# Three staging buffers moved and a new hand-made order in a fused attention, expert and channel-mix chain

## The chip, the cores and the metric

The kernel runs on one core of one Trainium2 chip. The metric is device time in microseconds of one execution; lower is better. Three executions of the kernel before took 497.76, 499.23 and 499.36 us, so the median is 499.23 us. One more execution was recorded by the hardware profiler, and all rows below are from that one.

## What is computed

Three blocks run one after the other on four sequences. The first is attention with 8 heads: 512 local tokens that see a window of 32 on each side and 32 global tokens, and 32 global tokens that see everything. Its output (576 tokens of 512 features) feeds four causal attention experts with a top-2 gate. Their sum feeds a channel mix with a sigmoid gate:

```python
x = concat(out_g, out_l)                       # block 1
logits = x @ w_gate                            # block 2: top-2 of 4 experts
q, k, v = x @ wq[e], x @ wk[e], x @ wv[e]
ye = softmax(causal(scale * q @ k.T)) @ v @ wo[e]
out += mask[..., None] * w[:, :, kk:kk+1] * ye
xk = mu_k * x + (1 - mu_k) * x_prev            # block 3
xr = mu_r * x + (1 - mu_r) * x_prev
k = maximum(xk @ w_k, 0)
result = sigmoid(xr @ w_r) * (k * k @ w_v)
```

## The kernel before

Products that need more than one pass of TensorE's rounded float are done with operands split into a high and a low half (H and L), three matmuls for one (`mm3`, line 161 and after). The halves are made by a copy on ScalarE or VectorE (the high half) and a subtraction on GpSimd or VectorE (the low half).

Block 1 has 32 units `n`, two for each of 16 pairs of heads. A unit is: `a_qk` (line 289) with sixteen matmuls `S`, four reductions on VectorE and four exponentials on ScalarE; `a_norm` (line 319) with a reciprocal `rc` on VectorE and three multiplications on GpSimd that make `pn` and `glob`; `a_tp` (line 338) with four transposes `pT` and a copy of them. Four units make a group `u`; `a_pv` (line 423) forms the group's output `x{u}0` and `x{u}1` with the values `vw`, and two groups are one sequence, held in `xT[b]`. The global queries are in `g_qk` and its followers (`Sga`, `Sgb`, `pTG`, `pTh`, `xg`, `pTx`). Inputs of a pair come as one `kq` tile, four of which fit.

Block 2 starts with projections. `load_wb` (line 239) fetches raw wq, wk and wv into a staging tile, and `split_wb` (line 250) makes their halves. `b_split` (line 448) makes the halves of `xT[b]` in a tile with the tag `x`; `b_qk` and `b_v` (lines 464 and 493) then do the projections, `pb{b}{ep}{q or k}{half}` and `pv{b}{i}`. All three raw tiles and the halves of `xT[b]` have the tag `x`, which has one buffer, so each of them has to be used up before the next can be fetched or written. After that come score tiles `C`, transposes `cT` and outputs `y`.

Block 3 folds the output weights into w_k and w_r (`g_make`, line 755: `Gr` and `Gk`), where the raw w_k and w_v arrive in quarter tiles through three staging tags in turn (`load_half`, line 221: tags `ql`, `mask`, `csm1`) and are split by `narrow_block` (line 188). The gate's sigmoids are computed early (`r`, `rl`) and parked in DRAM as `rd0` to `rd16`. Then four passes of `d_k` (tiles `k`, halves `kk`) and `d_v` (tiles `v`) run, and `d_out` (line 851) fetches a parked sigmoid into a tile `ro{n}{i}`, multiplies it with `v{n}{i}` and writes the product out. The last pass has five such tiles; they use the tags `wy` and `wg` by turns, with two buffers each, so three of the five share the two buffers of `wy`.

Nothing is scheduled by a library. Every call is recorded, and `Log.emit` (line 99) replays the record in the sequence of the table `ORDER`; the table `SLOTS` says which buffer of its tag, and which of the eight PSUM banks, each tile gets. So each engine executes its instructions in the sequence of that table, and a tile waits for the readers of the tile that had its buffer before. Every instruction has line 105, that of the replay.

Of the kernel before, what the change touches and what calls it, by code (L numbers as in the profile page):

```python
# [19 lines left out]
DM = H * HD  # L20
# [5 lines left out]
NC = DM // 128  # L26
# [91 lines left out]
def chain_kernel(ctx: ExitStack, tc: tile.TileContext, kq, vw, vgd, wqkv, wo, pack, w_k, w_v, w_r, c_causal, out):  # L118
# [82 lines left out]
    wy = {"n": 0}  # L201
# [649 lines left out]
    def d_out(n, i, pv):  # L851
        r = T(("wy", "wg")[i % 2], [DM], f"ro{n}{i}")
# [151 lines left out]
def sequence(text):  # L1004
    n = 0
    for word in text.split():
# [8 lines left out]
15 -7 12 -11x2 -14 10 2 -13 -2 26x6 -15 -10 7 -15 22 -22 10 3 -19 16 -5 -10x2 -4 19 576 -577 90 -29x8 1703 -1733x8 120  # L1015
-163x9 1 -2 -21 22 189x8 -196 -4 20 -20 2x8 -34 24 10 1 -2 2 11 -14 14 65 -80 14 37x8 -44 -6 19 1 -21 21 -35 101x8 -96
21 -20 -27 24 117x8 -124 92 3 -85 -13 39 68 -64 99 -103 -44 12 27 32x8 -35 -33 131 -100 -32 72 -63 20 -8 55 -59 53
-37x8 -16 -5 171 -168 47 -8 -121 123 3 -33 41 -41 -2 2 28 115 -152 -44x4 44 -54 83 -84 53 -73 124 -83 79 -105 8 92
-20x4 20 33 -141 103 31 -23x5 22 -141 29x4 -29 84 17 -3 11x4 -13 -25 -52 75 25 -15 -78 65 47x32 -50 -18 -13 30 -43 35
-12 -56 72x2 -71 115x2 -47 -40 43 -5x2 5x4 35 -42 61 -66 48x8 -53 61 -58 72x8 -97 63 1 -71 77 -7 8x4 -134 149 256x8  # L1020
-310 22 5 16 -23 28 -41 4 44x4 -111 97 -4 15x3 -12x4 -13 195x8 -234 27 7 -41 36 3 196 1 -206 23x8 -25 201 -212 208
-361 211x8 -100 107 -64 156x8 -224 122 -37 28 7 -40 31x2 6 -38 -3 -6 1 -2 43 -48 34 -31 4 30 -24x4 -21 20 -10x4 -6 28
-24 161x8 -151 -25 136 -126 128 -166 156 -120 127 -166 157 -125 127 -204x4 38 -39x3 300x8 -68 -50 9 42 -111x40 -87 -52
156 114 -90 28 -47 111 -66 -27 86 -79x8 -40 -24 -4 46 19 -39x4 -28 65 -153x4 155 -46 9 151 -195 74 -154 155x4 -77 -5
114x4 -16 -29 -55 170 -53 -60 -160x32 48 67 -177 246 -43 -29 -6 34 40 -138 113 -20 42 4 -10 -30x4 22 7 273 -352 81 -53
117x4 200 -270 -37 -161x2 146 116 -201 115 58x8 -57 -41 40 -41 -150 189 79x8 -279 301 -122 101 -133 151 -7x4 -153 136
# [36 lines left out]
122 60 -61x2 2 -3 2 -3 2x2 -48 84x2 10 -96 11 73x2 539 -629 47x12 -13 38 13 532 -537 140 -9 -209 -21 236 -90x3 -64 -66
129x3 -56 -42 208 -249 -2 132 4x4 108 -375 -2 127 605 -762x12 391 359 -2 -359 -375 733 -471 110 -258 -101x12 133 -182
144 608 -617 617 -464 -72 -173x12 232 -275 202 -176 -48 275 -229 41x12 652 -694 232 -233 233 459 -653x12 -14 192 -193
322x2 -243 185x4 53 -246 194x6 -198 188 -195 5 235x2 -241 199 -42x4 -231 308 -78 -232 248x4 15 -204 167 -69x6 59 -160
219x6 -44 -83 1 85 -88 96 -164x12 142 -87 122 -281 252 -27 54 -2 -227x12 161 55 -286 229 -129 183 -3 -54 -129 128
# [43 lines left out]

SLOTS = {
    "vC": "010100101",
    "kp": "10320321023120130123",
    "blk": "120102120120120",
    "bank": (
        "050534124535534141120326706341754527434545237344417313235256072171150256716757622557117214376540"
# [101 lines left out]
```

## Time and profile before

| | us |
|---|---|
| median of 3 executions | 499.23 |
| the profiled execution | 496.65 |
| its span, first to last instruction | 494.8 |
| TensorE busy in it | 470.3 (95%) |
| VectorE, ScalarE, GpSimd busy | 311.8, 284.1, 265.8 |
| bytes moved by DMA | 48.4 MB |

TensorE is busy for 95% of the span at a mean granted clock of 0.998 of full speed. The busy time counts modelled ends of matmuls, so short waits can hide in it. The other engines are busy for 54% to 63% of the span, but not evenly: for the first third they are close to full, and for the last quarter nearly empty.

### The profile page before, as it was taken

The page shows a single profiled execution, that of the slowest core. Times are in us where ns is not written, and L with a number is a line of the kernel's source. Part 1 is how long each engine was busy: PE and PEld are TensorE (multiplying, and loading weights), DVE is VectorE, ACT ScalarE, POOL GpSimd, SP SyncE. Part 2 cuts the span into 40 slices and gives each one's busy share as a digit, 9 for nine tenths or more (in the row PEclk, how much of TensorE's full clock was granted, in tenths as well). Part 3 has the DMA queues.
Part 4 walks back from the last instruction along what each step waited for, and adds up shares of the span by engine and source line. Part 5 has one row for each costly group of instructions (what it writes and reads, how often), then busy time and mean ns, then how long its engine had stood idle before and what let it go on. Part 6 is the DMA issues. An engine that isn't in the chain of part 4 may idle for free.

```text
span 494.8 us, 11667 instructions
## 1 busy us (share of the span) xinstructions
PE 470.3 (95%) x4238; PEld 399.3 (81%) x4238; DVE 311.8 (63%) x1126; ACT 284.1 (57%) x863; POOL 265.8 (54%) x389
## 2 busy tenths in 40 slices
PE   6798989999999999999999998998999999999994
PEld 5466778887988897997777786987989889989883
DVE  3887857997597667788767659987735125314222
ACT  4988986786567567668755756565422213214210
POOL 2978767476738756875856125686451332223240
PEclk9999999999999999999999999999999999999999
DMA  8947770040200000101022574412215013004003
GB/s 328 411 154 259 273 290 31 2 143 12 86 1 2 1 2 3 44 2 42 23 66 83 194 253 150 144 51 86 84 46 167 1 56 116 0 1 149 23 0 127
DMA packets 19369, 48.36 MB, mean 98 GB/s; under 512 B 2160, under 2 KB 2800, under 8 KB 19312
## 3 DMA queue, kind: packets, MB, share of 16 engines
q1 hardware_dynamic: 19024, 47.36, 27.5%
q8 instruction: 33, 0.54, 0.5%
q10 hardware_dynamic: 288, 0.26, 0.2%
q14 instruction: 24, 0.20, 0.1%
HBM read 38.70 MB, written 8.91 MB: 96 GB/s over the span
## 4 chain that ended last, share of the span: by engine, by line
PE 68%; DMA 11%; DVE 9%; ACT 4%; POOL 3%; issue 2%; SPq 0%; DVEq 0%; POOLq 0%; ACTq 0%
PE v L105 17%; DMA kq<-in_kq_dram 5%; PE pv L105 5%; PE cT L105 4%; PE y L105 4%; PE C L105 4%; PE x L105 3%; DMA rawk<-in_moe_w_k_dram 2%; PE S L105 2%; DMA vw<-in_vw_dram 2%; DVE rawv L105 2%; POOL wv L105 1%; PE pT L105 1%; DMA rawv<-in_moe_w_v_dram 1%; DVE rawk L105 1%
## 5 line engine op out<-in xcount | busy, mean ns | idle before, releaser
L105 PE MATMUL v<-wv,kk 128*128 128x512 f32 x408 | 98.0, 391 | 1.5 <-POOL wv L105 1.5
L105 POOL TENSOR_TENSOR kk<-k,kk 128x512 fp32r<-128x512 f32 (+1 forms) x32 | 44.9, 1410 | 87.2 <-ACT kk L105 82.6
L105 PEld LDWEIGHTS v<-wv,kk 128*128 128x128 f32 x408 | 74.9, 188 | 16.0 <-POOL wv L105 1.8
L105 ACT ACTIVATE sm<-sm,mn 128x160 f32<-128x160 f32 x128 | 53.6, 423 | 10.2 <-DVE mn L105 9.9
L105 POOL TENSOR_TENSOR pn<-sm,rc 128x256 f32<-128x256 f32 x64 | 38.6, 626 | 22.1 <-DVE mng L105 8.4
L105 ACT CAST kk<-k 128x512 fp32r<-128x512 f32 (+1 forms) x32 | 20.6, 649 | 50.7 <-PE v L105 37.1
L105 POOL TENSOR_TENSOR csm<-csm,crc 128x128 f32<-128x128 f32 (+3 forms) x64 | 46.9, 754 | 1.3
L105 DVE CUSTOM_DVE_ANT_0 sm<-S,band 128x160 f32<-128x160 f32 x128 | 35.6, 317 | 19.1 <-PE S L105 16.7
L105 ACT ACTIVATE csm<-csm,cmn 128x256 f32<-128x256 f32 (+3 forms) x64 | 35.9, 562 | 9.8 <-DVE cmn L105 5.9
L105 DVE TENSOR_TENSOR ro<-v,ro 128x512 f32<-128x512 f32 x17 | 11.6, 690 | 42.3 <-PE v L105 39.6
L105 DVE SCALAR_TENSOR_TENSOR k<-k 128x512 f32<-128x512 f32 (+1 forms) x32 | 28.7, 911 | 14.1 <-ACT k L105 13.5
L105 DVE CUSTOM_DVE_ANT_0 csm<-C,causal 128x128 f32<-128x128 f32 (+3 forms) x64 | 29.6, 486 | 6.4 <-PE C L105 2.5
L105 PE MATMUL S<-kq 64*64 64x160 f32 x512 | 25.2, 306 | 5.5 <-DMA kq<-in_kq_dram 3.8
L105 PEld LDWEIGHTS S<-kq 64*64 64x64 f32 x512 | 17.4, 132 | 14.0 <-DVE rc L105 3.9
L105 POOL TENSOR_TENSOR wk<-yk,wk 128x256 fp32r<-128x256 f32 x16 | 12.7, 797 | 29.3 <-ACT wk L105 29.3
L105 POOL TENSOR_TENSOR x<-xT,x 128x256 fp32r<-128x256 f32 (+1 forms) x32 | 22.4, 726 | 10.6 <-ACT x L105 10.6
L105 PE MATMUL pv<-wv,x 128*128 128x260 f32 x192 | 25.2, 286 | 0.0
L105 ACT ACTIVATION_READ_ACCUMULATOR sm<-sm,mn 128x1 f32 x128 | 24.6, 192 | 0.0
L105 PEld LDWEIGHTS pv<-wv,x 128*128 128x128 f32 x192 | 23.7, 188 | 0.7 <-DVE cmn L105 0.4
L105 PE MATMUL cT<-ident,csm 128*128 128x128 f32 x160 | 23.7, 279 | 0.0
L105 POOL TENSOR_TENSOR wv<-yv,wv 128x256 fp32r<-128x256 f32 x16 | 16.8, 1066 | 12.4 <-ACT wv L105 9.1
L105 PE MATMUL C<-qk 64*128 64x384 f32 (+3 forms) x192 | 22.4, 349 | 0.0
(901 smaller groups left out, 1270.8 us busy)
## 6 DMA issues: line engine op xcount, KB each, us to landing
kq<-in_kq_dram SPq DMA_DIRECT2D x15, 688.0 KB, 7.6
vw<-in_vw_dram SPq DMA_DIRECT2D x16, 512.0 KB, 10.5
ro<-rd SPq DMA_DIRECT2D x17, 256.0 KB, 2.9
rawk<-in_moe_w_k_dram SPq DMA_DIRECT2D x16, 256.0 KB, 3.5
rd<-rt SPq DMA_DIRECT2D x16, 256.0 KB, 3.5
rawv<-in_moe_w_v_dram SPq DMA_DIRECT2D x16, 256.0 KB, 2.7
out_dram<-ro SPq DMA_DIRECT2D x16, 256.0 KB, 2.1
rawr<-in_moe_w_r_dram SPq DMA_DIRECT2D x4, 512.0 KB, 3.8
```

Of the source, the lines that this page charges most:

```text
L105: getattr(getattr(self.nc, engine), name)(*[now(x) for x in args], **{k: now(x) for k, x in kwargs.items()})
```

## The change

Two tiles change their tag, and the two tables are replaced as a whole. The matmuls, the operations of the other engines and the DMAs are the same in number and kind.

```diff
-        raw = T("x", [NC, w], f"raww{kind}")
+        raw = T(("x", "d3", "qk")[step], [NC, w], f"raww{kind}")
...
-        r = T(("wy", "wg")[i % 2], [DM], f"ro{n}{i}")
+        r = T(("wy", "wg", "wy", "wg", "ql")[i], [DM], f"ro{n}{i}")
...
 ORDER = """
-15 -7 12 -11x2 -14 10 2 -13 -2 26x6 -15 -10 7 -15 22 -22 10 3 -19 16 -5 -10x2 -4 19 576 -577 90 -29x8 1703 -1733x8 120
+0 14 -14 19 -10 -13 26x6 -7 -14 -3 -2 4 -14 16 -15 11 -14 15 -18 2 17 -18 8 -9 9 582 -580 -14 106 -29x8 -29x8 21 1 -2
...
 SLOTS = {
-    "kp": "10320321023120130123",
+    "kp": "20310123132032101320",
```

The tag `d3` is otherwise used by the raw w_r and by a tile of block 3, `qk` (three buffers) by a transposed tile of block 1 and by the projections, `ql` by a small tile of block 2 and by the raw w_k and w_v. On the DMA queue of SyncE, raw wv is now the twelfth transfer instead of the 27th, ahead of the second round of `kq` tiles, and raw wk the 29th instead of the 20th.

The first place is TensorE's queue between the transposes of the global weights `pTg2` and the unit `S16`, the first that reads a tile of the third round of `kq`. Before (`pT` and `pTg` are transposes, `x1` the output of group 1):

```order
L105 MATMUL pT10_842<-ident_90,pn10_741 128x128 x4
L105 MATMUL pTg2_850<-ident_90,glob2_666 128x128 x4
L105 MATMUL x10_866<-pt1_513,vw2_203 64x64 x16
L105 MATMUL x11_883<-pt1_513,vw2_203 64x64 x16
L105 MATMUL pT11_922<-ident_90,pn11_839 128x128 x4
L105 MATMUL pT13_936<-ident_90,pn13_909 128x128 x4
L105 MATMUL x10_866<-tg1_680,vgb_145 128x512
L105 MATMUL x11_883<-tg1_680,vgb_145 128x512
L105 MATMUL S16_0_951<-kq8_823 64x160
```

And now, where `pb` and `pv` are projections of the first half of sequence 0:

```order
L105 MATMUL pTg2_898<-ident_137,glob2_719 128x128 x4
L105 MATMUL pb00q0_909<-x00_744,wq_304 128x256 x12
L105 MATMUL pT10_929<-ident_137,pn10_865 128x128 x4
L105 MATMUL pb01q0_942<-x00_744,wq_304 128x256 x12
L105 MATMUL pT11_968<-ident_137,pn11_894 128x128 x4
L105 MATMUL pv01_976<-wv_490,x00_744 128x260 x12
L105 MATMUL pT13_998<-ident_137,pn13_966 128x128 x4
L105 MATMUL pv00_1004<-wv_490,x00_744 128x260 x12
L105 MATMUL pTG11_1036<-ident_137,gl_114 128x128 x4
L105 MATMUL pTG10_1048<-ident_137,gl_114 128x128 x4
L105 MATMUL pTh10_1056<-ident_137,gl_114 128x128
L105 MATMUL pTh11_1059<-ident_137,gl_114 128x128
```

The next row there is `S16`. Four projections, 48 matmuls, have come in between units of block 1; they stood after `S24` and later. The outputs `x10` and `x11` stand ahead of this piece now.

The second place is TensorE's queue where the folded weights `Gk` end and the first `k` tiles begin, in block 3. `Gk01` is read by the `c` matmuls, `Gk0s` by the `a` matmuls. Before:

```order
L105 MATMUL Gk011_5075<-wk00_4711,wok_4600 128x512 x6
L105 MATMUL Gk011_5075<-wk02_4705,wok_4600 128x512 x3
L105 MATMUL Gk011_5075<-wk03_4593,wok_4600 128x512 x3
L105 MATMUL Gk01s_5105<-wk00_4711,wos_3783 128x512 x6
L105 MATMUL Gk01s_5105<-wk02_4705,wos_3783 128x512 x3
L105 MATMUL Gk01s_5105<-wk03_4593,wos_3783 128x512 x3
L105 MATMUL k00c_5137<-dH0_3063,Gk01_5089 128x256
```

Now, on the same engine (of `r31c`, `r30a` and `r31a` the second halves, which read alike, are left out, and of `Gk01s` the last two rows):

```order
L105 MATMUL Gk011_5014<-wk03_4552,wok_4720 128x512 x3
L105 MATMUL r31c_5044<-Gr01_4324,dH3_4354 128x512 x2
L105 MATMUL r31c_5044<-Gr01_4324,dL3_4439 128x512
L105 MATMUL r30a_4834<-Gr00_4560,dH3_4354 128x512 x2
L105 MATMUL r30a_4834<-Gr00_4560,dL3_4439 128x512
L105 MATMUL Gk00s_5069<-wk00_4694,wos_4314 128x512 x6
L105 MATMUL Gk00s_5069<-wk02_4766,wos_4314 128x512 x3
L105 MATMUL Gk00s_5069<-wk03_4552,wos_4314 128x512 x3
L105 MATMUL r31a_4976<-Gr00_4560,dH3_4354 128x512 x2
L105 MATMUL r31a_4976<-Gr00_4560,dL3_4439 128x512
L105 MATMUL Gk01s_5106<-wk00_4694,wos_4314 128x512 x6
L105 MATMUL k01c_5140<-dH0_3151,Gk01_5031 128x256
```

Between the last matmul of `Gk011` and the first `c` matmul stood one group of twelve 128x512 matmuls; now there are two such groups (`Gk00s`, `Gk01s`) and three groups of six (`r31c`, `r30a`, `r31a`).

The third place is the end of SyncE's DMA queue. Before:

```order
L105 DMA ro30_6530<-rd12_81 128x512
L105 DMA ro33_6540<-rd15_84 128x512
L105 DMA ro34_6550<-rd16_85 128x512
L105 DMA out_0_dram<-ro23_6194 128x512
L105 DMA ro31_6614<-rd13_82 128x512
L105 DMA out_0_dram<-ro30_6530 128x512
L105 DMA out_0_dram<-ro31_6614 128x512
L105 DMA out_0_dram<-ro33_6540 128x512
L105 DMA ro32_6800<-rd14_83 128x512
L105 DMA out_0_dram<-ro34_6550 64x512 x2
L105 DMA out_0_dram<-ro32_6800 128x512
```

Now:

```order
L105 DMA ro33_6499<-rd15_84 128x512
L105 DMA out_0_dram<-ro23_6254 128x512
L105 DMA ro31_6645<-rd13_82 128x512
L105 DMA out_0_dram<-ro30_6470 128x512
L105 DMA out_0_dram<-ro31_6645 128x512
L105 DMA out_0_dram<-ro32_6488 128x512
L105 DMA out_0_dram<-ro33_6499 128x512
L105 DMA out_0_dram<-ro34_5660 64x512 x2
```

The fetch of `ro32` from among the last writes is gone: it now stands with those of `ro30` and `ro33`, while `ro34` is fetched into the tag `ql` as the 97th of the 133 transfers, between raw quarter tiles of w_v.

## Rows read from the trace of the kernel before

**Rows 1.** Stretches: us; PE, PEld, DVE, ACT, POOL busy; clock; DMA share; GB/s

```profile
0.00:47.00 47.00, 36.89 (x635) 26.61 (x639) 33.28 (x204) 38.45 (x151) 33.13 (x68) 1.00 0.75 282
47.00:120.00 73.00, 69.68 (x1203) 58.37 (x1196) 56.68 (x284) 57.12 (x211) 48.24 (x84) 1.00 0.38 141
120.00:300.00 180.00, 179.81 (x1352) 151.22 (x1351) 131.06 (x466) 122.25 (x350) 108.08 (x178) 1.00 0.18 57
300.00:360.00 60.00, 56.18 (x339) 49.66 (x338) 48.62 (x103) 34.44 (x86) 38.56 (x34) 1.00 0.31 101
...
487.80:494.80 7.00, 0.00 (x0) 0.00 (x0) 1.41 (x3) 0.00 (x0) 0.00 (x0) 0.86 0.48 163
```

**Rows 2.** Waits of PE: what waited for what, us in total, times, longest

```profile
PE S L105 <- DMA kq<-in_kq_dram: 3.8, 5, 1.1
PE k00c L105 <- POOL Gk L105: 1.6, 1, 1.6
...
PE v L105 <- POOL wv L105: 1.5, 1, 1.5
PE x L105 <- issue: 1.5, 1, 1.5
...
PE xg L105 <- ACT gl L105: 0.7, 1, 0.7
PE pTg L105 <- POOL glob L105: 0.6, 1, 0.6
```

**Rows 3.** Timeline of the end: start, us, engine, operation, tiles, count [idle before]

```profile
479.69 8.10 PE L105 MATMUL v<-wv,kk 128*128 128x512 f32 x35
...
487.14 1.37 DVE L105 TENSOR_TENSOR ro<-v,ro 128x512 f32<-128x512 f32 x2 [0.67 <-PE v L105]
488.29 0.38 SPq L105 DMA_DIRECT2D ro<-rd  x1
...
491.21 0.69 DVE L105 TENSOR_TENSOR ro<-v,ro 128x512 f32<-128x512 f32 x1 [2.69 <-DMA ro<-rd]
...
491.93 0.34 SPq L105 DMA_DIRECT2D out_dram<-ro  x1
```

**Rows 4.** DMA issues from 488.6 us: count, KB each, median us to landing

```profile
out_dram<-ro SPq DMA_DIRECT2D x2, 128.0 KB, 2.7
out_dram<-ro SPq DMA_DIRECT2D x1, 256.0 KB, 2.0
```

**Rows 5.** Timeline of PE from 43 to 47 us

```profile
43.35 1.09 PE L105 MATMUL pT<-ident,pn 128*128 128x128 f32 x8
44.37 1.13 PE L105 MATMUL x<-tg,vgb 64*128 64x512 f32 x4
46.63 0.64 PE L105 MATMUL S<-kq 64*64 64x160 f32 x12 [1.13 <-DMA kq<-in_kq_dram]
```

**Rows 6.** Timeline of PE from 60 to 70 us: the first projection

```profile
68.06 1.68 PE L105 MATMUL pb00k<-x,wk 128*128 128x256 f32 x12
```

**Rows 7.** POOL by shape, 0 to 47 us: busy, mean ns, idle before

```profile
L105 POOL TENSOR_TENSOR pn<-sm,rc 128x256 f32<-128x256 f32 x27 | 16.1, 616 | 10.3 <-DVE mng L105 8.4 <-DVE rc L105 1.4 <-ACT pt L105 0.5
L105 POOL TENSOR_TENSOR glob<-sm,rc 128x128 f32<-128x128 f32 x13 | 5.2, 403 | 0.0
L105 POOL TENSOR_TENSOR gl<-gl,rcg 128x544 f32<-128x544 f32 x4 | 4.4, 1097 | 0.8 <-DVE rc L105 0.8
L105 POOL TENSOR_TENSOR wq<-rawwq,wq 128x256 fp32r<-128x256 f32 x4 | 2.9, 734 | 0.0
```

**Rows 8.** Timeline of POOL: its first and last operations of that stretch

```profile
12.83 1.19 POOL L105 TENSOR_TENSOR pn<-sm,rc 128x256 f32<-128x256 f32 x2 [8.38 <-DVE mng L105]
...
43.61 0.40 POOL L105 TENSOR_TENSOR glob<-sm,rc 128x128 f32<-128x128 f32 x1
```

**Rows 9.** Timeline: PE's last Gk group, and POOL's low halves of w_v

```profile
303.42 2.88 PE L105 MATMUL Gk01s<-wk,wos 128*128 128x512 f32 x12
...
342.37 4.60 POOL L105 TENSOR_TENSOR wv<-yv,wv 128x256 fp32r<-128x256 f32 x3 [3.04 <-ACT wv L105]
```

More of the change, by code (lines that the diff above doesn't have):

```diff
@@ new lines @@
+2 -78 211x8 -141 -4 94 -94 -77 77 139 1555 -1555 -197x8 18 1 -2 170 -64 -107 2 103 -129 24 103 -126 138x8 312 -463 4
+-31x8 18 6 120 -124 14 169 -133x8 -65 127 -127 97x8 -25 -64 -34 196 -141 105 -163 163 -108 -41 148 16 -126 -64 153
+-30x8 -135 208 -206 61 72 -137 99x8 -38 -7 -67 138 -5 55 -58 -131 201 -50 -73 118 -69 -96 98 -4 -96 48 221 -241 -31 48
+221 -228 78 12x4 -42 -98 138 -88x4 54 -110 215 -162 -34x4 15 8 18 56 -79 22 -46 112x4 26 2 -124 15 151 -48 -128 129
+-31 27 -106 35x4 -62 77 -85 28 40 -3 67 70x4 -104 104 -206 134x32 39 -3 20 241 -242 241 -475 232 275 -438 17 148x4
@@ new lines @@
+-154 18 135 265 -420 179x4 -30 -3 -152 80x2 100 -243 -5 63 119x8 -190 62 81 -52 54x8 288 -351 48 49 -5 -95 157x8 -208
+137 -32 29 -94 66 -61x4 54 -67 97 -30 97 -101 4 96 -74 2 -30 100 47x40 -194 -4 230x8 -230 187 83 -332 152 178 -285
+206x8 74 -250 67 4 -52x8 253 -210 -5 106 -3 -104 2 105 -134x4 -89 215 -104 -25 -80x4 89 -106 115 -101 28x4 274 -275
+149x2 55x8 -187 382 1 -2 -193 -192 -4 196 -197 -8 9 193 -32 -173 173 -164 161 -173 50x32 -74 165 -93x2 -84 128 -129
+166 222 -219 -44 62 -192 214x8 -21 -120 64 101x8 -109 -68 69 239 -164 -56x8 -15 225 -4 -218 -24 74 4 35 52 -94 -33
@@ new lines @@
+-42x4 234 -263 17 42 -148x4 271 -119 -154 193x4 -115 10 54 -46 5 430x12 -403 3 60 -5 -56x4 56 10 -83 82 -31 453x12
+-518 82 -17 -54 59 3 -45 -85 124 -33x4 32 -50 4 319x12 -296 4 -30 -17 48 -15 76 -192 195x4 -84 163x12 -206 38 66 1200
+-1194 -8 -74 -34 1307 -1201 219 -192 9x4 217 940 -1309 203 -55 -38x4 20 67 -88 209 -178 216 -252 -31x8 -94 117 358
+-327 1153 -978x8 -335 476 -274x8 -115 38 -44 4x2 18x8 11 -43 -2 1212 -1261x32 17 7 -5 25 -446 448 -4x2 9 -7 -2 205
+-205 84 -140x2 135 -88 82 125 2 -122 -46 207x8 -49 -122 -46 158 -112 -143 256 -126 -36 211x8 -63 -295x4 353 -319 464
@@ new lines @@
+-137 100 96 34 -35 34 -32x12 -78 -100 161 -34 -258 90 233 -98 63 -292 256 -141 -117 103x3 150 66 -66 43 -158x12 100 1
+-75 -80 196 -118 137 -88 -44x12 -49 130 -51 -81 80 -14 -66 -3 2 -3 -93 282x3 -148 -138 19x12 -31 136 32 -119 -50 167
+112 -232 367x12 -314 -116 250 -136 138 -3 3 -2 -230 61x4 161 -227 65 44x4 286 -337 164 -26x2 -139 133x2 -89 196x4
+-200x2 285 -159x3 -219 287 84 -96x4 7 -71 67 -228 134 39x6 41 92 -375 177x6 -124 314 -371 -5 287x6 -234 124 55 -56
+404x6 -414 58 -4 192 -432 182 248 -432 618x6 -193 -195 358 -165 -142 -168 115 51 -165x10 -138 240 -240 292 298 -592
@@ new lines @@
+593 -594 291 -292 589 -590x3 619 -387 -70 -49 293x6 -255 126 -160 104 385 -386 53 -173 426x4 -430 171 -7 34 228
+-226x10 284 3x2 -338 337 -261 -154x4 119 216 -187 212 -242 241 -258 -17x12 48 -24 -21 44 -154 203 -99 -104 120 80
+-16x2 -115x12 -84 -5 101 88 -63 273 -301 47 40x2 -159x12 41 105 -194 87 111 -199 330 -182x12 37 133 -332 41 230 -231
+206x3 -93 113 -307x12 415 -121 -23 -139 -2 281 -120 -117 92x3 -140 302 -405x12 -48 138 156 144 -441 275 94x4 66 -261
+260 23x3 -284 189 94x3 -290 182x4 -183 -2 -140 480x4 -162 -323 133 94x4 -93 208x10 66 58 -64 -189 -98 258 -93x6 50 130
@@ new lines @@
+134x6 -140 -49 211x13 -36 -2 251x6 -139 -83 -36 89 33x7 -95 -87x6 175 -24 23 -274x12 24x3 31 -32x3 29 -30x6 55x2 243x6
+-249 86x6 -92 -35x3 123 -92 174 -208x9 24x3 31 -32x3 29 -30x6 85x6 -33 -35x3 65 -34 -33x3 342x6 -348x3 345 -346x3
+133x6 210x6 -215 -117x3 329 -314x6 251x6 -251 1 -31x3 276 36x6 -291 -29x3 26 295 -323x3 321 -160x7 -27 -119x15 104
+-102x3 -5 41 -35x3 -5 36 -43 49x6 -45 -6 144x6 -95 -51 51 122x6 37x6 -43 104 -286x3 226 -109 101x6 -85 -93 -49 298
+-123x6 43 -226 47 177 99x6 -40 8x6 -119 -79x6 36 -104x3 65x2 -67x3 231 -232x6 121x6 -69 26x6 37 -70 69 255x6 -299
@@ L1109 @@
+33 -34x9 25x18 3x3 -5 7x3 -5 -6 12x3 -5 -6 12x3 -5 -6 10 -6 5x2
 """
@@ L1140 @@
-    "qk": "012011120102120",
+        "210020110212201002021010121200200121012120210002212200011002210102002012001011021222201010210100"
+        "12101201002112"
+    ),
+    "cpt": "10010101011010011010011010",
+    "mng": "10011001",
+    "sug": "01101001",
+    "wg": "01000000110001011011011001101011001",
+    "rcg": "01101001",
+    "qk": "1020122020120102",
     "lg": "0000",
     "gate2": "0101",
-    "cmn": "01202100120121102202210102100122",
-    "csu": "01202100210212022112001210200211",
@@ L1145 @@
-    "crc": "02101202101201202102011210200211",
+    "cmn": "00121020202101100212002112012201",
+    "csu": "02101012201001222201001221202120",
+    "crc": "01202012101010222210220110210102",
 }
```

189 lines of the change are left out of this document (77 added, 112 removed).

## The prediction

> **What bounds the kernel now.** I read the table of stretches first. It says that TensorE sets the time nearly everywhere: between 120 and 300 us it idles for 0.2 of 180 us, and between 360 and 487.8 us not at all, at a granted clock of 1.00 [rows 1]. The idle time stands in four places: 47.00 − 36.89 = 10.1 us in the first 47, 73.00 − 69.68 = 3.3 up to 120, 60.00 − 56.18 = 3.8 between 300 and 360, and the last 7.0 us, in which TensorE has nothing left [rows 1]. That is 24.4 us in all, and since the change removes no instruction, it is all that a new order can win. The list of TensorE's waits names the parts: 3.8 us for `kq` transfers in five waits, 1.6 for GpSimd's half of `Gk`, 1.5 for a half of w_v, and 0.6 and 0.7 for the global weights [rows 2]. The timeline shows the end: the last matmul group starts at 479.69 and runs 8.10 us, to 487.79; VectorE's two products are over at 487.14 + 1.37 = 488.51; then VectorE stands still for 2.69 us, released by the transfer that brings a parked sigmoid, makes one more product until 491.90, and the last write is issued at 491.93 [rows 3].
>
> **The tail.** The product that comes last in time is not that of the last matmul; it is `ro32`, whose fetch was issued only at 488.29 [rows 3], because it shares two buffers with `ro30` and `ro34`, and a write had to empty one first. Now `ro34` has a buffer of another tag and `ro32` is fetched with `ro30` and `ro33`, so the wait of 2.69 and the product of 0.69 behind it have no reason left. The last thing is then the write of `ro34` in two halves behind the products that end at 488.51. The old end was 494.8: issue at 491.93, a landing 2.0 us after it [rows 4], and 0.9 until the span's end. The new end at best: two issues at 0.34 us, 2.0 to land, 0.9 after it, so 488.51 + 0.1 + 0.7 + 2.0 + 0.9 = 492.2, minus what the second issue overlaps with the first landing, about 0.3: 491.9. At worst the halves take the 2.7 us that halves took here [rows 4], with 0.2 more at each issue: 492.9. So the gain is 1.9 to 2.9; I take **2.4**, since the halves before ran beside a fetch and a 256 KB write and these will run alone. On what halves cost, the row says that 128 KB took 2.7 us where 256 KB over all partitions took 2.0 [rows 4]. The Trainium skill, page "SBUF — State Buffer", section "Door 1: The DMA port swizzle (why `[64,N]` ≈ `[32,N]`)", has it that 64 neighbouring partitions reach half of the ports, so that a half tile isn't written faster than a whole one; by that rule the gain is the 1.9 end, and the row doesn't speak against it.
>
> **The front.** Raw w_v has a buffer of its own and is fetched twelfth, so projections stand between units of block 1. What they remove: TensorE waited 1.13 us at `S16` for the third round of `kq` [rows 5]. Ahead of that unit there are now four projections of twelve matmuls and some transposes more. Eight transposes take 1.09 us [rows 5], these about 0.8. Twelve projection matmuls take 1.68 us [rows 6], so four take 6 to 6.7, several times the wait: gain **1.1**. Bytes ahead of `kq4` are nearly unchanged (raw w_v is in, part of the values is out), so the second round should land as before; nothing is taken for it. The rest of the idle time of this stretch, 10.1 − 3.8 = 6.3 us [rows 1, 2], waits on the first softmaxes: GpSimd's first `pn` starts at 12.83, after 8.38 us without work, behind the reductions of VectorE [rows 8]. In the new order nine reductions stand ahead of the first reciprocal instead of about fifteen, so GpSimd should begin up to 3.0 us earlier. I take a third of the 6.3 for it, **2.1** (bounds 0 and 3.2).
>
> What it costs: GpSimd was nearly full from 12.83 to 43.61 + 0.40 [rows 8]. Its work up to `pn13`, the unit in front of `S16`, is now 26 `pn` (0.616), 12 `glob` (0.403), 3 `gl` (1.097), and twelve subtractions that make low halves, four each of wq, wv and the first half of `x` (0.734, that of wq [rows 7]): 16.0 + 4.8 + 3.3 + 8.8 = 32.9 us. Before, 16.1 + 5.2 + 4.4 + 2.9 = 28.6 us of work [rows 7] took the 31.2 from 12.83 to 44.01, a factor of 1.09. So 32.9 us become 35.8, and `pn13` is done at 45.6 if it starts at 9.8, and at 48.6 if it starts at 12.83 again. TensorE was there at 43.35; now three of the projections (4.9 us) and the 1.13 us group of `x10` and `x11` stand ahead [rows 5], so it comes at 49.4, or at 47.3 if the 2.1 is won. The cost is 0 to 1.3 (a late start with the 2.1 won in another way); I take **0.3**, near the early start, since that is what the 2.1 assumes. Of the operations of VectorE and GpSimd that run beside each other, rows show two things: 27 `pn` at a mean of 616 ns in the crowded front [rows 7], and a group of three low halves of w_v that took 4.60 us, or 1.5 each, at 342.37 [rows 9]. The Trainium skill, page "SBUF — State Buffer", section "SBUF: two separate sides", calls the port pair of the two engines an exclusive lock for a whole instruction; the second row fits that, the first doesn't need it, and it speaks against bringing subtractions forward, which is a rival below. One more cost: the outputs `x10`, `x11` now share a PSUM bank with a transpose just ahead of them. No row shows such a wait; the nearest are the two for one operation of ScalarE or GpSimd, 0.7 and 0.6 [rows 2]; I take **0.4** (0 to 0.7). Front: 1.1 + 2.1 − 0.3 − 0.4 = **2.5**, bounds −0.9 (none of the 2.1, all of both costs) and 4.3.
>
> **From 47 to 120 us.** The 3.3 idle us are single waits, the longest for no visible releaser (1.5) [rows 2]. `pb00k0` at 68.06 was the first projection [rows 6], so up to there no projection could stand where a unit waits; now they stand among the units from the front on. I take a quarter of the idle time, **0.8** (0 to 3.3).
>
> **The `Gk` stage.** The `c` matmuls waited 1.6 us for GpSimd's half of `Gk` [rows 2], with one group of twelve 128x512 matmuls, 2.88 us, between [rows 9]. Now there are two such groups and three of six, 5 × 1.44 + 2.88 = 10.1 us. That covers the old distance, 2.88 + 1.6, twice over: gain **1.6**. The wait of 1.5 for w_v [rows 2] comes from GpSimd's long operations in front of it [rows 9]; nothing in the order there changes that, so I take 0 (0 to 1.5), and the other 0.7 of the stretch's 3.8 I leave.
>
> **Elsewhere.** From 120 to 300 us there is nothing to win (0.2 us), and every wait there is new. Some PSUM banks are reused after a shorter distance than before. No row shows the price; the nearest are single waits of 0.6 to 0.7 [rows 2]. I take **−0.5**, bounds 0 and −4 (six such waits).
>
> **Sum.** 2.4 + 2.5 + 0.8 + 1.6 − 0.5 = **6.8** us off the profiled execution of 496.65, whose span is 494.8. It lies 2.58 under the median of 499.23, a profiled one among runs from 497.76 on, so I take the gain off the median: 499.23 − 6.8 = **492.4**.
>
> **The rivals.**
> Tail alone. The change doesn't do in the front what it says: the four projections fill the wait for `kq8`, but GpSimd, which makes four halves of w_v and of `x` more by then, hands `pn` over later by as much, and TensorE's idle time only moves. For it: GpSimd was busy 33.13 of the first 47 us [rows 1], nearly all of it in one piece. Against it: 6.5 us of TensorE's work to cover eight low halves more, 5.9 us of GpSimd's. Then only the tail remains, 499.23 − 2.4 = 496.8; with the `Gk` wait, 495.2.
>
> GpSimd becomes the bound, slower than before. Place: `pT13` and the units after it, ahead of `S16`. If GpSimd's operations are held by VectorE's as the three of 342.37 were, 1.5 us rather than 0.73, 32.9 us of work swell. The gains outside the front, with the 1.1 at `S16`, are 2.4 + 0.8 + 1.6 − 0.5 + 1.1 = 5.4, so the change ends slower if `pn13` comes more than 5.4 us after TensorE's 49.4, later than 54.8. From a start at 12.83 this is a factor of 42.0 / 32.9 = 1.28 in place of 1.09. At 1.35 `pn13` is done at 57.2, TensorE loses 7.8, and the time is 499.23 − 5.4 + 7.8 = 501.6. Against it is the 616 ns of 27 `pn` beside a busy VectorE [rows 7].
>
> The gains are given back between 120 and 300 us: with six new waits of 0.7 and the front at nothing, 499.23 − 2.4 − 1.6 + 4 = 499.2, no change.
>
> **How the numbers follow.** My forecast (gains in at least two of the three places, 488.5 to 495) has 0.60, at 492.4; tail alone (495 to 497.7) 0.17; no change 0.11; GpSimd the bound 0.12. A measurement of this kernel tells 0.3%, 1.5 us, from no change. Faster than 497.7 is then 0.60 + 0.16 = 0.76, within 0.3% 0.12, slower 0.12. The range runs from 488.5, which takes the upper bounds of the front and the middle and leaves about 0.04 below, to 498.0, above the tail alone; the slower case and most of no change are outside, 0.2 in all with those below.
>
> **What would show it.** In the profile after: the last gap of VectorE gone and the end about 4 us behind the last matmul rather than 7; no wait of `S` for `kq` at `S16`; the first `pn` before 11 us; no `c` matmul waiting for `Gk`; `S16` at 46.63 + 6.5 + 0.8 − 2.5, about 51.4; about 0.7 between 120 and 300. The forecast is wrong if `pT` waits for `pn` by several us before `S16`, or if TensorE's busy time itself rises, or if idle time shows up between 120 and 300 us.

## The result and the profile after

The changed kernel takes 478.55 us in the median (478.0 to 478.8, four executions); the kernel before took 498.78 in the same comparison (497.76 to 499.36). The ratio is 0.9595, with an interval of 0.9575 to 0.9615. So the kernel is faster, as forecast, but by 20.2 us where I forecast 6.8: 492.4 is 13.9 us too long, and 478.55 lies below the whole range. Four executions among those of the next sections were in a slow state (502 to 2,584 us) and are left out of every median and ratio.

Of the profiled executions the one before took 496.65 us and the one after 478.80. The head of the page after gives the span, and busy time and share of each engine (the numbers of before: span 494.8, PE 470.3 (95%), PEld 399.3, POOL 265.8):

```profile
span 477.0 us, 11651 instructions
PE 464.5 (97%) x4238; PEld 401.9 (84%) x4238; DVE 313.1 (66%) x1126; ACT 284.3 (60%) x863; POOL 261.1 (55%) x389
```

The stretches of after, with the columns of [rows 1]:

```profile
0.00:47.00 47.00, 40.15 (x662) 31.92 (x663) 34.16 (x209) 39.38 (x157) 35.83 (x71) 0.96 0.87 331
47.00:120.00 73.00, 72.69 (x1286) 63.27 (x1285) 56.76 (x302) 60.22 (x215) 50.82 (x85) 1.00 0.33 117
120.00:300.00 180.00, 179.19 (x1302) 153.70 (x1302) 142.07 (x470) 127.24 (x364) 112.08 (x182) 1.00 0.21 67
300.00:360.00 60.00, 60.00 (x376) 54.19 (x376) 43.81 (x88) 29.21 (x72) 31.74 (x29) 1.00 0.29 89
...
470.00:477.00 7.00, 2.43 (x11) 1.69 (x9) 3.16 (x5) 0.00 (x0) 0.00 (x0) 0.87 0.56 187
```

TensorE's waits of after, as in [rows 2] (what waited for what, us in total, times, longest):

```profile
PE S L105 <- DMA kq<-in_kq_dram: 2.1, 3, 1.0
PE pT L105 <- POOL pn L105: 1.8, 2, 1.3
```

The span fell by 17.8 us. The two lists and [rows 1] split that into three parts. The time behind the last matmul went from 7.0 to 7.00 − 2.43 = 4.6, which is 2.4. The idle time of TensorE ahead of it went from 10.1 + 3.3 + 0.2 + 3.8 = 17.4 to 6.85 + 0.31 + 0.81 + 0 = 8.0, which is 9.4; the waits for `Gk`, for a half of w_v, for the global weights and the 1.5 us of `x` for no visible releaser are off the list. And TensorE's **busy** time went from 470.3 to 464.5, which is 5.8, with the same 4238 matmuls. The clock doesn't explain it: in the first 47 us it was 1.00 before and 0.96 after, in the three stretches up to 360 us 1.00 in both, and a slower clock only adds busy time, here at most 47 × 0.04 = 1.9 us to that of after. The forecast had nothing for that third part. (The stretches are cut by time, so the same row doesn't hold quite the same work in both kernels; the sums aren't touched by that.)

### The profile page after: what moved, and what is told of

It is laid out like the page before. It is cut to its first block, busy times and chain, and to the rows that moved or that the text cites. A ratio compares the mean times of both kernels' runs of the same rounds, so it can differ in the third digit from the quotient of the medians.

```text
span 477.0 us, 11651 instructions
## 1 busy us (share of the span) xinstructions
PE 464.5 (97%) x4238; PEld 401.9 (84%) x4238; DVE 313.1 (66%) x1126; ACT 284.3 (60%) x863; POOL 261.1 (55%) x389
## 4 chain that ended last, share of the span: by engine, by line
PE 86%; DVE 6%; ACT 5%; DMA 1%; issue 1%; POOL 0%; SPq 0%; DVEq 0%; POOLq 0%; ACTq 0%
PE v L105 19%; PE x L105 5%; PE pv L105 4%; PE y L105 4%; PE C L105 3%; ACT sm L105 3%; PE cT L105 3%; PE S L105 2%; PE Gk L105 2%; PE pT L105 2%; DMA kq<-in_kq_dram 1%; DVE csm L105 1%; ACT csm L105 1%; PE xg L105 1%; DVE sm L105 1%; PE pb30q L105 1%
## 5 line engine op out<-in xcount | busy, mean ns | idle before, releaser
L105 POOL TENSOR_TENSOR kk<-k,kk 128x512 fp32r<-128x512 f32 (+1 forms) x32 | 43.8, 1370 | 88.7 <-ACT kk L105 72.9
L105 ACT ACTIVATE csm<-csm,cmn 128x128 f32<-128x128 f32 (+3 forms) x64 | 35.7, 560 | 8.8 <-DVE cmn L105 7.6
L105 PE MATMUL pv<-wv,x 128*128 128x260 f32 x192 | 26.5, 288 | 0.0
L105 PE MATMUL cT<-ident,csm 128*128 128x128 f32 x160 | 25.5, 276 | 0.5 <-POOL csm L105 0.3
L105 PE MATMUL S<-kq 64*64 64x160 f32 x512 | 23.3, 317 | 2.3 <-DMA kq<-in_kq_dram 2.1
L105 PEld LDWEIGHTS S<-kq 64*64 64x64 f32 x512 | 18.6, 140 | 7.9 <-issue 3.5
L105 POOL TENSOR_TENSOR wk<-yk,wk 128x256 fp32r<-128x256 f32 x16 | 13.1, 826 | 19.6 <-ACT wk L105 17.5
L105 POOL TENSOR_TENSOR crc<-crc,gate 128x2 f32<-128x2 f32 x32 | 7.1, 233 | 29.6 <-DVE crc L105 22.9
```

The source lines that it names most:

```text
L105: getattr(getattr(self.nc, engine), name)(*[now(x) for x in args], **{k: now(x) for k, x in kwargs.items()})
```

## Where busy time can go when no work goes

The same matmuls took longer before, so I looked at what one and the same group takes from its start to the start of the next. In the order before, units and transposes alternate. Timeline of TensorE, kernel before (start, us, operation, tile of the array used, shape, count):

```profile
26.13 0.66 PE L105 MATMUL pT<-ident,pn 128*128 128x128 f32 x4
26.72 0.77 PE L105 MATMUL S<-kq 64*64 64x160 f32 x16
27.43 0.66 PE L105 MATMUL pTG<-ident,gl 128*128 128x128 f32 x4
```

In the order after, they stand in rows of their own kind. Timeline of TensorE, kernel after:

```profile
56.06 1.52 PE L105 MATMUL pT<-ident,pn 128*128 128x128 f32 x12
57.42 0.60 PE L105 MATMUL pTg<-ident,glob 128*128 128x128 f32 x4
57.95 1.86 PE L105 MATMUL S<-kq 64*64 64x160 f32 x48
59.74 1.32 PE L105 MATMUL xg<-vw,gl 128*32 128x64 f32 x80
...
63.01 0.33 PE L105 MATMUL pTx<-ident,xq 128*128 128x128 f32 x1
63.18 0.60 PE L105 MATMUL pT<-ident,pn 128*128 128x128 f32 x4
63.71 1.13 PE L105 MATMUL x<-tg,vgb 64*128 64x512 f32 x4
64.77 2.33 PE L105 MATMUL S<-kq 64*64 64x160 f32 x48
```

Before, four transposes cost 26.72 − 26.13 = 0.59 and a unit 27.43 − 26.72 = 0.71: 1.30 us. After, twelve transposes cost 57.42 − 56.06 = 1.36, so four cost 0.45, and three units cost 59.74 − 57.95 = 1.79, so one costs 0.60: 1.05 us. The 0.25 us between them are two changes, from matmuls on the whole array (128*128) to matmuls on a part of it (64*64 here; the 64*32, 64*128, 128*64 and 128*32 of other tiles count as parts too) and back: some 0.12 us a change. None of it shows as idle time in these rows, since the matmuls' records cover it.

Counted in the trace's records of TensorE, in order of start, there are 106 such changes before and 64 after. Changes between two sizes of part are not in this count; there are 30 of them before and 31 after, so they can't make the difference. At 0.12 to 0.16 us, 42 fewer make 5.0 to 6.7 us; the busy time fell by 5.8, or 0.14 each. The Trainium skill, page "TensorEngine Tiling (Array Packing)", section "Key Properties", says it in a sentence: "Mode switching requires drain: Changing tiling mode (not just tile) drains the TensorE". The rows fit that, and the price of some 0.12 us is theirs.

So the theory is: what I missed is changes of array mode, some 0.14 us each. Its rival: busy time is what matmuls cost, and the 5.8 us belong to something else in the new order, such as shorter waits inside groups, so that putting changes back costs little or nothing.

## The experiments

All times are medians; +x is against after's 478.55. The kernel before had medians of 498.0 to 498.8 beside the various runs, so differences of some tenths of a microsecond between runs say nothing.

**More changes, the theory's main test.** In the changed kernel parts of groups that were ready anyway are exchanged at 24 places between 50 and 240 us, so that there are 110 changes in place of 64. One place of TensorE's order, of 24:

```
-L105 MATMUL pT_1242<-ident,pn_1026 128x128 x4
-L105 MATMUL pTg_1252<-ident,glob_1019 128x128 x4
-L105 MATMUL S_0_1260<-kq_903 64x160
...
+L105 MATMUL pT_1242<-ident,pn_1026 128x128 x2
+L105 MATMUL S_0_1245<-kq_903 64x160
...
+L105 MATMUL pT_1242<-ident,pn_1026 128x128 x2
+L105 MATMUL pTg_1263<-ident,glob_1019 128x128 x4
```

> The kernel after with one edit: at 24 places between 58 and 238 us, the last two to six matmuls of a run of whole-array matmuls (128*128) and the first two to six of the run of part-array matmuls behind it (64 rows or 64 columns), or the other way round, change places on TensorE. Everything else keeps its order. Changes between the two sorts rise from 64 to 110; in the kernel before there are 106. Theory 1 (changes cost time): in the traces the start of the next matmul comes about 0.20 us after the start of the last one at such a change, against 0.14 between two different whole-array groups and 0.04 to 0.08 between part-array matmuls; per change that is about 0.16 us net, 46 x 0.16 = 7: 485.5 us (483 to 487). Theory 2 (TensorE's busy time fell because short waits for operands hide under modelled ends, and a change costs nothing): no operand comes later, so 478.5 to 479.5.

Measured: 489.62 us, 0.9849 of before (0.9819 to 0.9879), +11.1 us, more than the 487 at which the theory's range ended. Where the time went is read from one more execution of the same kernel.

> The kernel of e1_more_changes once more, for a trace. Theory 1: TensorE's busy time is 6 to 8 us above that of the kernel after, and the idle time within 1 us of it; about 0.20 us from start to start at each change. Theory 3 (delayed operands): 4 us or more of e1's 11 stand as idle time or as starts right behind a release.

Measured: 489.92 us. All 46 added changes lie between TensorE's first matmul of `S16` and its first of `Gk01s`, a stretch with the same matmuls in both kernels. First in after, then in this run, with the columns of [rows 1]:

```profile
49.30:292.53 243.23, 242.11 (x2514) 207.86 (x2514) 189.37 (x750) 178.94 (x557) 155.64 (x260) 1.00 0.23 76
50.23:303.47 253.24, 251.46 (x2514) 207.77 (x2514) 189.62 (x750) 178.95 (x557) 155.73 (x260) 1.00 0.22 73
```

The stretch is 10.0 us longer, at a clock of 1.00 both times, and 251.46 − 242.11 = 9.35 us of that are busy time; idle time grew by 0.7. So the rival is out: putting changes back costs, and as busy time. That is more than the 6 to 8 us expected. 9.35 over 46 changes is 0.20 each, above the 0.14; but here groups were cut into pieces as well, and a piece can cost on its own.

**Half as many changes put back.** The same with 12 of the exchanges, 88 changes:

```
-L105 MATMUL x_1385<-pt_1024,vw_810 64x64 x16
-L105 MATMUL pTx_1424<-ident,xq_1405 128x128
-L105 MATMUL pT_1426<-ident,pn_1238 128x128 x4
+L105 MATMUL x_1385<-pt_1024,vw_810 64x64 x10
+L105 MATMUL pTx_1401<-ident,xq_1399 128x128
+L105 MATMUL pT_1403<-ident,pn_1238 128x128 x3
+L105 MATMUL x_1385<-pt_1024,vw_810 64x64 x6
+L105 MATMUL pT_1403<-ident,pn_1238 128x128
```

> As e1_more_changes, with every second of its exchanges: 12 exchanges, changes between whole-array and part-array matmuls 64 to 88. Theory 1 (each change costs, as the rows say, about 0.16 us): 24 x 0.16 = 3.8, 482.4 us; if e1's own price holds (11.2 us for 46, 0.24 each), 5.8, 484.4. Half of e1's loss is expected in either case, spread over the changed places in the trace, in TensorE's busy time and not in its idle time. Theory 3 (the exchanges delay operands, and e1 measured waits): the trace shows idle time of TensorE, or starts right behind a release, at the exchanged places, and the loss need not be half.

Measured: 485.4 us, 0.9747 (0.9721 to 0.9773), +6.9 us or 0.29 a change. The cost grows with the number of exchanges; half of them cost somewhat more than half (6.9 of 11.1). No trace shows how much of this is busy time.

**Changes between whole groups only.** Now hardly any group is cut: 17 exchanges of whole groups, 98 changes in place of 64. Two of the places:

```
+L105 MATMUL S_0_1252<-kq_903 64x160
...
-L105 MATMUL pTg_1252<-ident,glob_1019 128x128 x4
+L105 MATMUL pTg_1265<-ident,glob_1019 128x128 x4
...
-L105 MATMUL pT_1426<-ident,pn_1238 128x128 x4
 L105 MATMUL x_1368<-tg_1285,vgb 128x512
 L105 MATMUL x_1385<-tg_1285,vgb 128x512
+L105 MATMUL pT_1428<-ident,pn_1238 128x128 x4
```

> The kernel after with 17 exchanges at the same sort of place as e1, but of whole groups (a transposed tile, a projection, a unit's scores, an output) instead of pieces of two to six matmuls, so that hardly any group is cut in two: changes 64 to 98. What it tells apart: if the price stands at the change itself, as in the rows of before and after (0.20 from start to start there, net 0.14 to 0.16 each), 34 of them cost 4.8 to 5.4 us, 483.6; if e1's 0.24 is the price of a change, 8.2 us, 486.7; if e1 and e5 paid for the cutting of groups alone, 478.5 to 479.5.

Measured: 484.43 us, 0.9726 (0.9665 to 0.9788), +5.9 us. First the same stretch, from `S16` to `Gk01s`, then a piece of TensorE's timeline in this run, over the groups shown above for after:

```profile
48.89:297.49 248.60, 247.69 (x2514) 207.28 (x2514) 189.87 (x750) 178.85 (x557) 155.23 (x260) 1.00 0.22 74
```

```profile
55.61 1.52 PE L105 MATMUL pT<-ident,pn 128*128 128x128 f32 x12
57.06 0.77 PE L105 MATMUL S<-kq 64*64 64x160 f32 x16
57.77 0.66 PE L105 MATMUL pTg<-ident,glob 128*128 128x128 f32 x4
...
62.87 0.33 PE L105 MATMUL pTx<-ident,xq 128*128 128x128 f32 x1
63.13 1.13 PE L105 MATMUL x<-tg,vgb 64*128 64x512 f32 x4
64.19 0.66 PE L105 MATMUL pT<-ident,pn 128*128 128x128 f32 x4
64.77 1.62 PE L105 MATMUL S<-kq 64*64 64x160 f32 x32
```

From the first row to the last this takes 64.77 − 55.61 = 9.16 us; in after the same groups took 64.77 − 56.06 = 8.71. The 0.45 us are the four added changes, 0.11 each. Over the whole stretch, which holds all 34, busy time rose by 247.69 − 242.11 = 5.6 us, 0.16 each (0.17 by the medians), close to the 0.14 of the 42 changes between before and after. So the price at a change of mode is 0.11 to 0.17 us. What the two runs before cost beyond that came with cutting groups into pieces; by what mechanism, I did not find out. (In this run there are also 16 more places in the stretch where one tile's matmuls end and another's begin, 324 for 308; no run tells what these cost by themselves.)

**Fewer changes in the kernel before.** The other way round, 94 in place of 106 changes, with everything else of the kernel before:

```
+L105 MATMUL pTh_1771<-ident,gl 128x128
+L105 MATMUL pTG_1773<-ident,gl 128x128 x4
-L105 MATMUL S_0_1771<-kq_1212 64x160
...
-L105 MATMUL pTh_1790<-ident,gl 128x128
-L105 MATMUL pTG_1792<-ident,gl 128x128 x4
```

> The kernel before with one edit: six pairs of neighbouring runs on TensorE (a whole-array run and a part-array run of 3 to 12 matmuls each, such as cT and C) change places, so that runs of a sort join: 106 changes become 94. Everything else keeps its order. Theory 1: 12 x 0.16 to 12 x 0.24 less, 1.9 to 2.9 us, 495 to 496 where before has 498. Theory 2 (a change costs nothing): 498, or more if an operand comes late.

Measured: 496.88 us against 498.1, ratio 0.9981 (0.9952 to 1.0011). The sign fits, but the interval holds no change at all, so the time neither supports nor refutes the theory. The traces say a little more: from `S16` to `Gk01s`, with the same matmuls and a clock of 1.00, TensorE is busy for 253.27 us before (46.63 to 303.41) and for 252.13 here (46.74 to 303.28). That is 1.14 us for 12 changes, 0.10 each, while idle time grew from 3.5 to 4.4 us and took most of it back. The next kernel, with as many changes as before, has 253.63 us in that stretch, so 0.4 of this is within what such a comparison can tell.

**The tail alone.** The kernel before with only the last five buffers and the DMA order of after:

```diff
-        r = T(("wy", "wg")[i % 2], [DM], f"ro{n}{i}")
+        r = T(("wy", "wg", "wy", "wg", "ql")[i], [DM], f"ro{n}{i}")
```

> The kernel before with the tail of the new one alone: ro34 in the tag ql, ro32 fetched right behind ro30, its product and its write ahead of those of ro33. Nothing else moves. Theory (the tail's term of the prediction): 2.4 us less, 496.4 us, and the end 4.6 us behind the last matmul instead of 7.0. Rival (the two half writes of ro34 take the place of the late product): no change, 498 to 499. The wait of 1.5 us without a visible releaser at 63 us should be there again if it belongs to the order, and not if it came once.

Measured: 493.9 us against 497.98, ratio 0.9934 (0.991 to 0.9957), so 2.1 to 4.5 us faster. Its timeline shows the end:

```profile
483.66 5.83 PE L105 MATMUL v<-wv,kk 128*128 128x512 f32 x25
...
486.81 3.41 DVE L105 TENSOR_TENSOR ro<-v,ro 128x512 f32<-128x512 f32 x5 [9.32 <-PE v L105]
```

The last matmul ends at 489.49 and the span at 494.1, 4.6 behind it, as in after. The wait of 2.69 us of [rows 3] is gone. So the term of 2.4 holds on its own, without the rest of the change, for what comes behind the last matmul. The times differ by other amounts for reasons outside the tail: the medians by 4.1 us, and the profiled executions (495.88 and 496.65) by 0.8, since here the last matmul ended 1.7 us later than before (489.49 against 487.79).

**The `Gk` groups moved back.** In after, the three groups of six and `Gk00s` are moved behind the first `c` matmuls, so that only one group of twelve stands ahead of these, as before:

```
+L105 MATMUL Gk01s<-wk_4694,wos 128x512 x6
...
+L105 MATMUL k01c<-dH_3151,Gk_5031 128x256
...
 L105 MATMUL r31c<-Gr_4324,dH_4354 128x512 x2
...
 L105 MATMUL r31a<-Gr_4560,dL_4439 128x512
-L105 MATMUL Gk01s<-wk_4694,wos 128x512 x6
...
-L105 MATMUL k01c<-dH_3151,Gk_5031 128x256
```

> The kernel after with one edit: the groups r31c, r30a, Gk00s and r31a, which stand between Gk011 and the first c matmuls, come behind the first group of c matmuls. Between the last matmul of Gk011 and the first c matmul stands one group of twelve again, as in the kernel before. Theory (distance covers the wait for the halves of Gk): the wait comes back, 1.6 to 2.0 us, 480.3 us. Rival (the halves are made sooner in the new order of ScalarE and GpSimd, so the distance is not what removed the wait): 478.5.

Measured: 482.15 us, 0.9698 (0.9669 to 0.9727), +3.6 us. But not where I had the wait. Timeline of TensorE of this run, from the end of `Gk01s` on (idle time ahead of a group and its releaser in brackets):

```profile
288.30 0.28 PE L105 MATMUL k01c<-dH,Gk 128*128 128x256 f32 x1
...
300.45 0.39 PE L105 MATMUL k00a<-dH,Gk0s 128*128 128x256 f32 x1 [0.95 <-ACT Gk0s L105]
...
301.18 0.39 PE L105 MATMUL k00a<-dH,Gk0s 128*128 128x256 f32 x1 [0.22 <-DVE Gk0s L105]
...
303.02 0.58 PE L105 MATMUL k00a<-dH,Gk 128*128 128x256 f32 x1 [0.75 <-ACT kc L105]
```

The `c` matmuls start at 288.30 without a wait, behind a single group of twelve. So the longer distance is not what took away the 1.6 us. What differs is how soon the low half of `Gk` is made. ScalarE copies the finished `Gk` out, and GpSimd subtracts. In the kernel before, the last `Gk` matmul ended at 299.79 + 3.79 = 303.58; timelines of ScalarE and of GpSimd:

```profile
305.74 0.44 ACT L105 ACTIVATE yk<-rawk 128x256 f32<-128x256 f32 x1 [1.20 <-DMA rawk<-in_moe_w_k_dram]
...
306.38 0.57 ACT L105 CAST Gk<-Gk 128x512 fp32r<-128x512 f32 x1
306.86 0.58 ACT L105 COPY g0k<-Gk 128x512 f32<-128x512 f32 x1
307.52 2.97 POOL L105 TENSOR_TENSOR Gk<-g0k,Gk 128x512 fp32r<-128x512 f32 x2
```

In this run it ended at 284.62 + 1.07 = 285.69:

```profile
285.78 0.59 ACT L105 COPY g0k<-Gk 128x512 f32<-128x512 f32 x1 [0.20 <-ACT rt L105]
286.26 0.59 ACT L105 CAST Gk<-Gk 128x512 fp32r<-128x512 f32 x1
286.93 1.29 POOL L105 TENSOR_TENSOR Gk<-g0k,Gk 128x512 fp32r<-128x512 f32 x1 [1.51 <-ACT Gk L105]
```

Before, ScalarE reached the two copies 2.8 us after the last matmul: an operation on raw w_k stood ahead of them in its queue and waited 1.20 us for its transfer. GpSimd began at 307.52, right behind the second copy (306.86 + 0.58 = 307.44). Now the copies come at once, as in after (285.86), and GpSimd's half is over at 288.22. By these rows it is the order of ScalarE that took the wait away; no run moves that operation alone. What the moved groups do cover in after is the `a` matmuls: without them these wait 0.95 + 0.22 + 0.75 = 1.9 us. And with these waits TensorE's clock fell. A stretch of this run, with the columns of [rows 1]:

```profile
303.00:306.40 3.40, 3.38 (x16) 3.38 (x17) 2.77 (x9) 1.44 (x5) 0.81 (x1) 0.51 0.09 35
```

For 3.4 us the granted clock is at 0.51, near the lower of its two levels (1.2 of 2.4 GHz), which loses 3.4 × 0.49 = 1.7 us more. Together 1.9 + 1.7 = 3.6, and from `S16` on this profiled execution (483.0 us) took (481.2 − 49.6) − (477.0 − 49.3) = 3.9 us longer than that of after. That the median is +3.6 as well is partly chance: two of its executions, 481.92 and 482.39 us, had mean clocks of 1.000 and 0.999, which leaves no room for such a loss, and were 3.4 and 3.8 above 478.55 all the same. What they lost instead, no trace shows.

**The early projections moved back.** In after, the four projections ahead of `S16` are moved behind it, to the place ahead of `S18`:

```
 L105 MATMUL pTg_898<-ident,glob_719 128x128 x4
-L105 MATMUL pb00q_909<-x_744,wq 128x256 x12
-L105 MATMUL pT_929<-ident,pn_865 128x128 x4
-L105 MATMUL pb01q_942<-x_744,wq 128x256 x12
...
+L105 MATMUL pT_916<-ident,pn_865 128x128 x4
+L105 MATMUL pT_942<-ident,pn_894 128x128 x4
```

> The kernel after with one edit: the four projections pb00q0, pb01q0, pv01 and pv00, with the eight copies that read them, are moved from ahead of S16 to the gap ahead of S18, some 9 us later on TensorE; the fetch of raw w_v and its halves stay early. Theory A (as predicted: they cover one wait for the third round of kq): 1.1 us more, 479.7. Theory B (they also fill the waits of the units ahead of and behind S16 for their softmaxes, which the prediction put into a separate term): 3 to 6 us more, 481.5 to 484.5. If the units don't need filling at all: 478.5.

Measured: 485.15 us, 0.9759 (0.9729 to 0.9788), +6.6 us. That is above the 1.1 us of the wait for `kq` and a little above the 3 to 6 that the waits for softmaxes would give. The timeline of TensorE of this run:

```profile
42.43 1.23 PE L105 MATMUL pT<-ident,pn 128*128 128x128 f32 x8 [1.06 <-POOL pn L105]
45.69 0.66 PE L105 MATMUL pT<-ident,pn 128*128 128x128 f32 x4 [2.03 <-DVE pt L105]
46.18 1.67 PE L105 MATMUL pTG<-ident,gl 128*128 128x128 f32 x8
47.65 0.63 PE L105 MATMUL pTh<-ident,gl 128*128 128x128 f32 x2
```

And the same groups in after:

```profile
48.12 1.03 PE L105 MATMUL pTG<-ident,gl 128*128 128x128 f32 x8
48.99 0.38 PE L105 MATMUL pTh<-ident,gl 128*128 128x128 f32 x2
49.30 2.67 PE L105 MATMUL S<-kq 64*64 64x160 f32 x64
```

Without projections to do, TensorE waits for `pn` and for a copy `pt`, then does the same eight transposes in 47.65 − 46.18 = 1.47 us instead of 0.87 (the granted clock is 0.91 from 40 to 60 us). Idle time is 484.8 − 467.3 = 17.5 us in this run against 12.5, so 5.0 of the 7.8 us in the span are waits. The other 2.8 are busy time, with 64 changes as in after. The slow clock here is 20 × 0.09 = 1.8 of busy time, but after had a slow stretch of its own (0.96 in its first 47 us), so what the clock adds between the two is not shown. Moving the projections to the front is worth much more than the one wait at `S16`, mainly for the waits they fill.

## Why the prediction was wrong

The sign and the places were right. Its own steps, by the profiled executions:

| step | predicted, us | measured, us |
|---|---|---|
| tail | 2.4 | 2.4 |
| front, 0 to 47 us | 2.5 | 10.1 − 6.85 = 3.3 |
| 47 to 120 us | 0.8 | 3.3 − 0.31 = 3.0 |
| `Gk` stage, 300 to 360 us | 1.6 | 3.8 − 0 = 3.8 |
| 120 to 300 us | −0.5 | 0.2 − 0.8 = −0.6 |
| busy time of TensorE | 0 | 470.3 − 464.5 = 5.8 |
| sum | 6.8 | 17.7 |

**The step that failed** is the sentence on the 24.4 us of idle time: "since the change removes no instruction, it is all that a new order can win". Busy time isn't fixed by the instructions; it depends on which of them are neighbours. The new order has 42 fewer changes between whole and part array and 5.8 us less busy time, and the runs with changes put back show that such changes cost, and cost as busy time: at 0.10 to 0.17 us, 42 of them are 4 to 7 us. The rows were there: in [rows 5] the transposes stand at 128*128 and the unit at 64*64, and two places of one order can be compared start to start. The order of the change, too, shows which kinds stand side by side. I counted what waits, and not what alternates.

**Tail.** Right, in its mechanism too. The last product ends 0.7 us behind the last matmul, as [rows 3] let one expect, and the two halves land in 2.3 us:

```profile
467.73 4.70 PE L105 MATMUL v<-wv,kk 128*128 128x512 f32 x20
...
469.75 3.41 DVE L105 TENSOR_TENSOR ro<-v,ro 128x512 f32<-128x512 f32 x5 [19.07 <-PE v L105]
```

```profile
out_dram<-ro SPq DMA_DIRECT2D x2, 128.0 KB, 2.3
```

That lies between the 2.0 and 2.7 of [rows 4]. The rule of the Trainium skill that I weighed there, page "SBUF — State Buffer", section "Door 1: The DMA port swizzle (why `[64,N]` ≈ `[32,N]`)", by which 64 neighbouring partitions reach half of the ports, fits these rows: the halves took 2.3 us, no less than the 2.0 of a whole tile before.

**Front.** The signs that I named are there. GpSimd starts earlier and hands over `pn13` where I had it (45.6): timeline of GpSimd, kernel after, its first operation and the two `pn` that end at 45.55.

```profile
10.30 1.18 POOL L105 TENSOR_TENSOR pn<-sm,rc 128x256 f32<-128x256 f32 x2 [6.05 <-DVE rc L105]
...
44.36 1.19 POOL L105 TENSOR_TENSOR pn<-sm,rc 128x256 f32<-128x256 f32 x2
```

So the rival in which GpSimd becomes the bound is out: its point was 54.8. `S16` starts at 49.30 without a wait, 2.1 us ahead of the 51.4 of the forecast; `pT` waits 1.8 us for `pn` in after where it waited 1.2 before, and `x` for nothing, so the costs that I took for GpSimd and the PSUM bank, 0.3 and 0.4, came out at about 0.6 and 0. What was mis-sized is the value of the projections. I had them fill 1.1 us; moved back, they cost 6.6, of which the trace shows 5.0 as waits.

**47 to 120 us.** Mis-sized: I took a quarter of the 3.3 us, and nearly all of it went. The largest wait there, 1.5 of `x` with no visible releaser, stayed in the two kernels that keep the order of before (1.2 in the tail alone and in that with fewer changes) and is gone in after. I did not isolate it further.

**`Gk` stage.** The size was right for the `c` matmuls and the reason wrong: the run with the groups moved back shows that it is not the distance, and the rows there point to ScalarE's order. For the wait on w_v I wrote that nothing in the order in front of it changes, and took 0; it is gone. GpSimd's low halves of w_v, from the view of that tile between 260 and 380 us (duration in ns as least, median and most, then the first and the last start); before:

```profile
L105 POOL TENSOR_TENSOR wv<-yv,wv x16: 732/888/3021, 317.0 to 362.8; 128x256 fp32r<-128x256 f32 x16
```

After:

```profile
L105 POOL TENSOR_TENSOR wv<-yv,wv x16: 732/794/1191, 295.9 to 348.7; 128x256 fp32r<-128x256 f32 x16
```

They start 21 us earlier, while the kernel ends 17.8 us earlier, and none of them takes longer than 1.2 us, where one took 3.0 in before. Whether their length or their place made the difference, no run tells.

**The base.** I took the gain of the profiled execution off the median of 499.23. The profiled execution lay 2.58 us under that median, and after's lies 0.25 above its own. These 2.8 us and the 11.0 by which the sum was short make the 13.9.

**The range** had no case for busy time. Its lower end took the upper bounds of the front and the middle (with the other terms these add up to 11.1 us, which is 488.1 rather than 488.5). With 5.8 us of busy time it would have begun at about 482.7, which is still above the result; the rest is the wait for w_v, the other waits of that stretch and the base.

## What to carry to other kernels

Before an order is judged by TensorE's waits, count in it how often whole-array and part-array matmuls alternate, and price a change by comparing one group alone with the same group in a row, start to start; on this kernel it was 0.10 to 0.17 us, all of it inside busy time. Work that is ready at any time is worth most where the critical engine waits in several short pieces, and its value there is all of these, not the one longest wait. When a side engine hands a tile over late, follow the tile back through the engines that make it and look at what stands ahead of it in each one's queue, and only then at how far away its reader is.

## What the runs showed of the hardware that I had not expected

- A change between matmuls on the whole array and on a part of it cost 0.10 to 0.17 us between whole groups, and 0.20 where groups were cut in pieces (46 changes, 9.35 us of busy time at a clock of 1.00).
- Three waits of TensorE, none over 0.95 us and 1.9 us in all within 3.5 us, went with 3.4 us at a granted clock of 0.51, so they cost 3.6 in that execution.
- The spread of the kernel before goes in part with the clock. Of the executions on one chip one took 494.72 us at a mean granted clock of 0.996 and another 500.51 at 0.984: 5.8 us, where 0.012 of some 497 us is 6.0. But a third took 498.89 at 0.994, so the clock is not all of it. The kernel after, with fewer waits, stayed within 0.8 us at 0.994 to 0.999. That this is why its gain by medians (20.2) is larger than by the profiles (17.8) is an inference; no run takes the clock apart from the waits.
